# Attention and two dense layers in one program: the order of the first batch is planned anew

## The chip, the cores and the metric

One core of a Trainium2 chip runs the program. The metric is the device time of one execution in microseconds (us); lower is better. The engines are TensorE (PE; its weight loads are shown apart as PEld), VectorE (DVE), ScalarE (ACT), GpSimd (POOL) and the queue of SyncE (SP), which issues nearly all transfers.

## What is computed

The reference takes q, k and v of shape (4, 8, 576, 64), rotates q and k by position, and computes attention for each of 4 batches and 8 heads; its output, as 2304 rows of 512, goes through two dense layers of width 2048 with different gates:

```python
scores = scale * np.matmul(q_rot, k_rot.transpose(0, 1, 3, 2))
attn = np.exp(scores - np.max(scores, axis=-1, keepdims=True))
attn = attn / (np.sum(attn, axis=-1, keepdims=True) + 1e-09)
x = np.matmul(attn, v)              # then (B, S, H * D) as 2304 x 512
h = x @ w_in
x = (h * np.clip(h + 3.0, 0.0, 6.0) / 6.0) @ w_out      # layer 1
h = x @ w_in2
P = a[0] + a[1] * h + a[2] * h ** 2 + a[3] * h ** 3
Q = 1.0 + np.abs(b[0]) * np.abs(h) + np.abs(b[1]) * h ** 2
out = (P / (Q + 1e-06)) @ w_out2                         # layer 2
```

## The kernel before

Heads are handled in pairs, four pairs to a batch. For a pair, `prep_qk` loads q and k, bounds their size, rotates them (L796, L803, L806), splits them into a high and a low 16-bit half (L812) and transposes both by DMA on SP (tiles t0, t1); `prep_v` loads v and splits it (L747). A unit of attention (`unit`) is 128 query rows of both heads of a pair (64 rows of each in the last one). PE makes the scores s (L854), DVE takes the row maximum mx (L860), ACT the exponential e (L867); e is split into p16h (a copy on POOL, ACT or DVE, L537 to L541) and p16l (a subtract on DVE, L879), both are transposed by DMA (L876), and PE multiplies them with v into ob (L896, L899, "pv"). Units 0 and 1 of a pair are part 0 of the batch (256 rows), units 2 to 4 part 1 (320 rows). `x_out` divides by the sum, splits the rows (L923, L932) and transposes them into xt (L935).

Once all four pairs of a part are there, `layer1` runs: for each of 16 slices f of the hidden width 12 matmuls (L966), relu on ACT (L970), the product t on DVE (L972), its high half gh and low half gl (L975); then, for each of four output blocks, four pieces of 12 matmuls (L990) that need the splits of w_out for four slices f each. The weights of layer 1 come as raw float32: 16 slices of w_in and 16 of w_out are loaded (raw, L619 and L622), decoded into an exact scaled form (ACT L634, DVE L636, L637), bounded (L652) and split into two halves (L539 on POOL, L644 on DVE). One scale serves four slices of w_in; all of w_out has one, so no split of w_out can start before its last slice is loaded, decoded and bounded. The splits of w_out carry the name so in the rows. Layer 2 is decoded during the last batches and runs at the end (L1140, L1173).

Nothing of this is issued in the order in which it is written. Every step is an `Op` with a list of engines that may run it, a cost, a priority and its dependences. `Plan.order` plays the program through with these costs: whenever an engine is free it takes the ready step with the lowest priority number; a second choice of engine costs a penalty. The result is the order of instructions on each engine, and each engine then keeps to it. The priority of a step is a time in ticks that `at` sets, plus an offset of its class of tiles from the table `PR` (`o_`, and `z_` for the first batch alone):

```python
o.prio += PR.get("o_" + cls(o.nm[1:]), 0) * 4000
if self.first:
    o.prio += PR.get("z_" + cls(o.nm[1:]), 0) * 4000
```

The other entries of `PR` that matter here: `wi0`, `wi1`, `wo0`, `wo1` set the times at which slices of w_in and w_out are due, `l1o` and `l1p` those of layer 1, `c01` moves part 1 of batch 0, and the `e_` entries list the engines for a class of steps (D, A, G for DVE, ACT, POOL; those that end in 0 hold for the early batches).

Of the kernel before, what the change touches and what calls it, by code (L numbers as in the profile page):

```python
# [37 lines left out]
PR = {'c01': -11.047,  # L38
# [69 lines left out]
 'o_hx': 2.9,
 'o_ident': 123.38,
 'o_k2': 20.73,  # L110
 'o_lgh': 20.57,
 'o_lgl': -106.78,
 'o_lq': -26.42,
 'o_lr': -17.86,
 'o_ls': -32.38,
 'o_lt': 4.62,
# [10 lines left out]
 'o_pth': -0.49,
 'o_ptl': -17.99,
 'o_pw': 29.19,
 'o_pwi': -70.51,  # L130
 'o_qal': -46.2,
 'o_qam': -19.48,
 'o_qb': -31.25,
 'o_qk16': -0.07,
 'o_qpi': -4.09,
 'o_qps': 9.14,
 'o_qpv': -7.12,
 'o_r': -32.53,
# [1131 lines left out]
```

## Time and profile before

| | before |
|---|---|
| time, median of 3 runs | 1168.32 us (1166.86 to 1169.74) |
| profiled execution | 1166.88 us |
| its span, first to last instruction | 1165.1 us |
| mean granted clock of PE | 0.943 |
| busy PE / PEld | 989.7 us (85%) / 787.6 us (68%) |
| busy DVE | 946.6 us (81%) |
| busy ACT | 686.3 us (59%) |
| busy POOL | 227.4 us (20%) |
| DMA queue q1 (SP) | 54.1% of 16 engines' span |

A busy share is an average over stages that differ: where one engine is at 98% another may wait for it, and the roles change with the stage. So the table tells only which engines come into question. The rows further below cut the span at points of the program (the first matmul of layer 1, of its second half, of part 1, of batch 1).

### The profile page before, as it was taken

The page shows a single profiled execution, that of the slowest core. Times are in us where ns is not written, and L with a number is a line of the kernel's source. Part 1 is how long each engine was busy: PE and PEld are TensorE (multiplying, and loading weights), DVE is VectorE, ACT ScalarE, POOL GpSimd, SP SyncE. Part 2 cuts the span into 40 slices and gives each one's busy share as a digit, 9 for nine tenths or more (in the row PEclk, how much of TensorE's full clock was granted, in tenths as well). Part 3 has the DMA queues.
Part 4 walks back from the last instruction along what each step waited for, and adds up shares of the span by engine and source line. Part 5 has one row for each costly group of instructions (what it writes and reads, how often), then busy time and mean ns, then how long its engine had stood idle before and what let it go on. Part 6 is the DMA issues. An engine that isn't in the chain of part 4 may idle for free.

```text
span 1165.1 us, 21501 instructions
## 1 busy us (share of the span) xinstructions
PE 989.7 (85%) x8102; PEld 787.6 (68%) x8102; DVE 946.6 (81%) x1721; ACT 686.3 (59%) x1233; POOL 227.4 (20%) x271
## 2 busy tenths in 40 slices
PE   0222456989998999998999999989999999999997
PEld 0121235876677777777866787768888888888895
DVE  5879789889868789878894747689988889787887
ACT  4545633646446556464654634588776776676676
POOL 0343055433424223243231310000000000000000
PEclk9955566999999999999999999999999999999999
DMA  6888887788689787979889884721210010010010
GB/s 196 222 176 222 199 149 162 154 158 153 121 170 171 154 158 164 180 161 160 173 174 171 164 183 146 260 70 52 81 37 1 25 34 7 1 37 10 1 37 19
DMA packets 299048, 142.97 MB, mean 123 GB/s; under 512 B 246720, under 2 KB 280128, under 8 KB 298944
## 3 DMA queue, kind: packets, MB, share of 16 engines
q1 hardware_dynamic: 293456, 134.69, 54.1%
q10 hardware_dynamic: 5488, 6.92, 2.3%
q8 instruction: 63, 1.03, 0.4%
q14 instruction: 41, 0.34, 0.1%
HBM read 61.33 MB, written 17.83 MB: 68 GB/s over the span
## 4 chain that ended last, share of the span: by engine, by line
PE 53%; DVE 20%; DMA 10%; ACT 6%; issue 5%; SPq 3%; POOL 2%; ACTq 0%; DVEq 0%; POOLq 0%
PE ac L1173 15%; PE h L990 9%; PE hh L1140 9%; PE hx L1140 7%; PE h L966 7%; DMA ptl<-p16l 5%; DVE mx L860 4%; PE s L854 4%; DVE p16l L879 3%; ACT e L867 3%; DMA t<-qk 2%; PE ob L896 2%; DVE w L644 1%; DVE t L972 1%; DVE gl L975 1%
## 5 line engine op out<-in xcount | busy, mean ns | idle before, releaser
L966 PE MATMUL h<-xt,w 128*128 128x256 f16 (+1 forms) x1536 | 202.7, 287 | 8.6 <-DVE t L972 7.5
L990 PE MATMUL h<-gh,w 128*128 128x256 f16 (+1 forms) x960 | 190.6, 287 | 0.0
L1173 PE MATMUL ac<-w,lgh 128*128 128x512 f32 x576 | 179.3, 392 | 3.3 <-ACT lgh L1163 2.5
L966 PEld LDWEIGHTS <-w 128*128 128x128 f16 x1536 | 148.5, 98 | 49.6 <-issue 11.5
L867 ACT ACTIVATE e<-s,mx,qal 128x576 f32<-128x576 f32 (+1 forms) x144 | 116.0, 834 | 104.3 <-DVE p16l L879 49.0
L990 PEld LDWEIGHTS <-w 128*128 128x128 f16 x1440 | 139.3, 99 | 35.2 <-issue 0.3
L854 PE MATMUL s<-t,t 128*128 128x192 f16 (+9 forms) x360 | 88.3, 300 | 65.8 <-DMA t<-qk 28.9
L990 PE MATMUL h<-gl,w 128*128 128x256 f16 (+1 forms) x480 | 137.8, 287 | 0.0
L860 DVE TENSOR_REDUCE mx<-s 128x2 f32<-128x1152 f32 (+1 forms) x80 | 99.4, 1245 | 38.0 <-PE s L854 19.8
L854 PEld LDWEIGHTS <-t 128*128 128x128 f16 (+1 forms) x720 | 61.6, 109 | 100.6 <-issue 43.3
L1173 PEld LDWEIGHTS ac<-w,lgh 128*128 128x128 f32 x576 | 106.9, 188 | 28.1 <-ACT lgh L1163 4.0
L1140 PE MATMUL hh<-x,w 128*128 128x512 f32 (+1 forms) x516 | 117.7, 378 | 2.7 <-DVE lt L1155 2.7
L879 DVE TENSOR_TENSOR p16l<-e,p16h 128x1152 f16<-128x1152 f32 (+1 forms) x80 | 101.2, 1265 | 20.6 <-DMA ptl<-p16l 19.5
L1173 PE MATMUL ac<-w,lgl 128*128 128x512 f32 x288 | 113.0, 392 | 0.0
L1140 PEld LDWEIGHTS hh<-x,w 128*128 128x128 f32 x516 | 92.0, 190 | 23.2 <-DVE lt L1155 3.9
L970 ACT ACTIVATE t<-h,half,d 128x256 f32<-128x256 f32 (+1 forms) x128 | 74.9, 587 | 47.7 <-PE h L966 46.7
L1140 PE MATMUL hx<-x,w 128*128 128x512 f32 (+1 forms) x444 | 98.2, 370 | 0.0
L539 POOL TENSOR_SCALAR gh<-t 128x256 f16<-128x256 f32 (+1 forms) x95 | 66.2, 698 | 148.6 <-DVE t L972 143.7
L862 POOL TENSOR_SCALAR mx<-mx,qal 128x2 f32<-128x2 f32 (+1 forms) x75 | 53.4, 712 | 203.3 <-DVE mx L860 140.2
L1140 PEld LDWEIGHTS hx<-x,w 128*128 128x128 f32 x444 | 77.5, 188 | 16.0
L854 PE MATMUL s<-k,t 128*128 128x192 f16 (+9 forms) x360 | 85.2, 299 | 0.0
L896 PE MATMUL ob<-v,pth 128*128 128x65 f16 (+1 forms) x800 | 77.1, 200 | 7.2 <-DMA pth<-p16h 3.3
(132 smaller groups left out, 1938.4 us busy)
## 6 DMA issues: line engine op xcount, KB each, us to landing
raw<-in_moe_w_in_dram SPq DMA_DIRECT2D x32, 512.0 KB, 4.7
raw<-in_moe_w_out_dram SPq DMA_DIRECT2D x32, 512.0 KB, 4.3
w2d<-f SPq DMA_DIRECT2D x32, 256.0 KB, 4.3
w2s<-w2d SPq DMA_DIRECT2D x32, 256.0 KB, 2.8
out_dram<-ob SPq DMA_DIRECT2D x36, 128.0 KB, 2.4
vnat<-in_v_dram SPq DMA_DIRECT2D x16, 256.0 KB, 3.4
nat<-in_q_dram SPq DMA_DIRECT2D x32, 128.0 KB, 2.4
nat<-in_k_dram SPq DMA_DIRECT2D x32, 128.0 KB, 2.5
```

The lines of the kernel that those rows point to most:

```text
L539: pool.tensor_scalar(out, in_, scale, 0.0, ALU.mult, ALU.add)
L854: pe.matmul(sbank()[r0:r0 + m, x:y], lhsT=qq[:, q0:q0 + m], rhs=kk[:, kx:kx + y - x], start=(j == 0), stop=(j == 1))
L860: op("D", c_dve(n), lambda e: vec.reduce_max(mx()[:, 0, 0:g], sv().rearrange("p (g n) -> p g n", g=g), axis=AX.X), r=[s], w=[(mx, 0)])
L862: op(EN("e_mx"), {"D": 170, "G": 270}, lambda e: EL[e].tensor_scalar(mx()[:, 1, 0:g], mx()[:, 0, 0:g], al()[:, 1:2], float(LSH * np.log(2. ...
L867: op("A", c_act(n // g, 2, False), lambda e, h=h: act.activation(et()[:, h * (n // g):(h + 1) * (n // g)], sv()[:, h * (n // g):(h + 1) * ...
L879: op(EN("lo"), c_sub(n), lambda e: EL[e].tensor_tensor(lo()[:, 0:n], et()[:, 0:n], ph()[:, 0:n], ALU.subtract), r=es + [ph], w=[lo])
L896: pe.matmul(ob()[0:m, o:o + D + 1], lhsT=w, rhs=vv[:, 0], start=(z == 0 and j == 0), stop=(z == 1 and j == 4))
L966: pe.matmul(hp()[:, 0:N], lhsT=w[:, z, kk], rhs=xt()[:, kk, 0:N], start=(n == 0), stop=(n == 11))
L970: op("A", c_act(N, 2, False), lambda e, t=t, hp=hp, f=f: act.activation(t()[:, 0:N], hp()[:, 0:N], AF.Relu, bias=half(), scale=d()[:, f:f ...
L990: pe.matmul(yp()[:, 0:N], lhsT=w[:, s_, m * 128:(m + 1) * 128], rhs=gt()[:, f, 0:N], start=(f == 0 and z == 0), stop=(f == KF - 1 and z == 2))
L1140: pe.matmul(hp()[:, 0:n], lhsT=w[:, kk], rhs=xt()[:, kk, 0:n], start=(i == 0), stop=(i == 11))
L1173: pe.matmul(accs[j][i]()[0:m], lhsT=gt()[:, x:x + m], rhs=wt(), start=(f == 0 and z == 0), stop=(f == KF - 1 and z == 2))
```

## The change

The table `PR` has new values nearly throughout, two new entries, and the preparation of the first batch reads them. Pairs 1 to 3 of batch 0 were due 4 ticks apart and before pair 0's time; now all four pairs start at one time of their own, one `step0` apart. v of pair 0 (`s0`) is due early, not late. Part 1 of batch 0 is moved ahead by 1 tick instead of 11 (`c01`). The offsets `z_` of the first batch are new and nearer to zero. Some engine lists change: the maxima's scaling (`e_mx`) runs on POOL alone outside the early batches, v's copy (`e_v`, `e_v0`) has POOL or DVE as its first choice instead of ACT, layer 1's output (`e_y`) stays on ACT.

```diff
-PR = {'c01': -11.047,
+PR = {'c01': -1.023,
...
- 'e_hi': 'GAD',
+ 'e_hi': 'ADG',
  'e_hi0': 'ADG',
- 'e_mx': 'DG',
+ 'e_mx': 'G',
...
- 'e_v': 'AD',
- 'e_v0': 'AG',
+ 'e_v': 'DG',
+ 'e_v0': 'GAD',
...
- 'e_y': 'AD',
+ 'e_y': 'A',
...
+ 'lead0': 7.701,
...
- 's0': 11.806,
+ 's0': -13.557,
...
+ 'step0': 0.971,
...
         if b_ == 0:
-            at(0)
+            at(-PR["lead0"])
             prep_qk(0)
             at(PR["s0"])
             prep_v(0)
             for p in range(1, HP):
-                at(4 * p - PR["lead"])
+                at(PR["step0"] * p - PR["lead0"])
                 prep_qk(p)
                 prep_v(p)
```

What the planner makes of it is seen in the order of instructions. The new kernel's table is two lines longer, so a line of it has a number that is 2 higher: L974 there is L972 here.

The first place is DVE's list just ahead of the first product t of layer 1. Before:

```order
L922 RECIPROCAL r<-r 128x6
L919 TENSOR_TENSOR xf<-vqs,vpv 128x1
L923 TENSOR_TENSOR xu<-xu,r 128x6x64
L609 RECIPROCAL qps<-qpv 128x2
L747 SCALAR_TENSOR_TENSOR v_90<-vnat_85,vqs,v_90 128x10x64
L932 TENSOR_TENSOR xl<-xu,xh 128x384
L972 SCALAR_TENSOR_TENSOR t<-t,h 128x256
```

The same place now:

```order
L639 SCALAR_TENSOR_TENSOR w_9_1306<-raw,w_9_1306 128x512
L638 TENSOR_SCALAR w_10_1330<-w_10_1330 128x512
L639 SCALAR_TENSOR_TENSOR w_10_1330<-raw,w_10_1330 128x512
L974 SCALAR_TENSOR_TENSOR t<-t,h 128x256 x2
L977 TENSOR_TENSOR gl<-t,gh 128x256
L862 TENSOR_REDUCE mx<-s 128x2
L974 SCALAR_TENSOR_TENSOR t<-t,h 128x256
L638 TENSOR_SCALAR w_11_1387<-w_11_1387 128x512
L881 TENSOR_TENSOR p16l<-e,p16h 128x1152
```

Before, the first t stood behind x_out of part 1 of the first pair (r, xu, xl) and behind all 16 splits of w_out, the last of which is in the next fence. Now t comes while the slices of w_out are still being decoded (w_10 here), and no split of w_out stands ahead of it.

The second place is DVE's list at the last split of w_out (w_14). Before:

```order
L644 SCALAR_TENSOR_TENSOR w_11_1451<-w_12_961,so,w_11_1451 128x512
L541 COPY xu<-ob 128x130
L860 TENSOR_REDUCE mx<-s 128x1
L644 SCALAR_TENSOR_TENSOR w_12_1461<-w_13_986,so,w_12_1461 128x512
L932 TENSOR_TENSOR xl<-xu,xh 128x256
L796 SCALAR_TENSOR_TENSOR ropea<-nat,tab 128x18x32
L860 TENSOR_REDUCE mx<-s 128x2
L644 SCALAR_TENSOR_TENSOR w_13_1479<-w_14_996,so,w_13_1479 128x512
L605 TENSOR_SCALAR qpi<-ob 128x2
L879 TENSOR_TENSOR p16l<-e,p16h 128x1152
L644 SCALAR_TENSOR_TENSOR w_14_1524<-f_1007,so,w_14_1524 128x512
```

Now:

```order
L646 SCALAR_TENSOR_TENSOR w_11_2295<-w_12_1462,so,w_11_2295 128x512
L881 TENSOR_TENSOR p16l<-e,p16h 128x1152
L646 SCALAR_TENSOR_TENSOR w_12_2335<-w_13_1557,so,w_12_2335 128x512
L798 SCALAR_TENSOR_TENSOR ropea<-nat,tab 128x18x32
L862 TENSOR_REDUCE mx<-s 128x2
L646 SCALAR_TENSOR_TENSOR w_13_2357<-w_14_1585,so,w_13_2357 128x512
L805 TENSOR_TENSOR nat<-nat,tab 128x1152
L646 SCALAR_TENSOR_TENSOR w_14_2379<-f_1647,so,w_14_2379 128x512
L881 TENSOR_TENSOR p16l<-e,p16h 128x640
```

Before, the last splits stood ahead of the first t, among attention and the loads' scaling. Now they stand behind all 16 products t of part 0, between part 1's attention and the rotation of the next batch's q and k (ropea, nat).

The third place is SP's list, where loads of w_out (raw) end. Before:

```order
L935 DMA_TRANSPOSE xt_906<-xh 128x2x128
L935 DMA_TRANSPOSE xt_922<-xl 128x2x128
L622 DMA raw<-in_moe_w_out_dram 128x1024 x2
L876 DMA_TRANSPOSE ptl<-p16l 128x9x128
L622 DMA raw<-in_moe_w_out_dram 128x1024
L876 DMA_TRANSPOSE pth<-p16h 128x9x128 x2
```

Now, around the transposes xt of the fourth pair:

```order
L937 DMA_TRANSPOSE xt_766<-xh 128x2x128
L878 DMA_TRANSPOSE ptl<-p16l 128x9x128
L624 DMA raw<-in_moe_w_out_dram 128x1024
L937 DMA_TRANSPOSE xt_783<-xl 128x2x128
L624 DMA raw<-in_moe_w_out_dram 128x1024 x2
L878 DMA_TRANSPOSE pth<-p16h 128x9x128
L878 DMA_TRANSPOSE ptl<-p16l 128x5x128
```

The first of these fences shows the second pair's transposes (xt_906 and xt_922, high and low half) and the last three loads of w_out, which stood ahead of the third pair's. Now the fourth pair's transposes (xt_766, xt_783) come while w_out is still loaded; six of its loads stand behind them, between transposes of p16h and p16l.

## Rows read from the trace of the kernel before

**Rows 1.** The page's slices: PE's busy tenths and its granted clock, in 40 equal parts.

```profile
PE   0222456989998999998999999989999999999997
...
PEclk9955566999999999999999999999999999999999
```

**Rows 2.** Windows by stage: length, busy us (count) of each engine, PE clock, DMA share, GB/s.

```profile
0.00:189.50 189.50, 57.78 (x499) 41.97 (x499) 149.39 (x289) 91.61 (x185) 62.51 (x67) 0.68 0.79 192
189.50:225.70 36.20, 34.08 (x398) 28.20 (x397) 33.98 (x69) 21.41 (x43) 17.34 (x24) 0.96 0.83 153
225.70:265.00 39.30, 34.53 (x406) 28.80 (x403) 34.23 (x55) 19.79 (x35) 14.27 (x13) 1.00 0.84 154
265.00:338.00 73.00, 68.82 (x747) 50.94 (x746) 60.42 (x109) 37.69 (x67) 26.98 (x30) 1.00 0.80 148
338.00:690.00 352.00, 330.57 (x3779) 263.85 (x3777) 276.39 (x520) 193.62 (x324) 103.95 (x136) 1.00 0.86 168
690.00:1165.10 475.10, 463.87 (x2288) 373.86 (x2286) 392.21 (x683) 322.23 (x581) 2.40 (x3) 0.99 0.19 52
```

**Rows 3.** Timeline of PE: start, us, instruction; the firsts of L966, L990, part 1, batch 1.

```profile
189.54 4.34 PE L966 MATMUL h<-xt,w 128*128 128x256 f16 x24
...
225.71 0.27 PE L990 MATMUL h<-gh,w_s 128*128 128x256 f16 x1
...
264.94 0.30 PE L966 MATMUL h<-xt,w 128*128 128x320 f16 x1
...
337.88 1.47 PE L966 MATMUL h<-xt,w 128*128 128x256 f16 x12
```

**Rows 4.** Windows, 30 to 190 us.

```profile
30.00:190.00 160.00, 56.90 (x498) 41.10 (x499) 133.53 (x241) 78.69 (x156) 62.58 (x64) 0.62 0.81 191
```

**Rows 5.** Groups, first 189.5 us: busy us, mean ns | idle before, releaser.

```profile
L637 DVE SCALAR_TENSOR_TENSOR w<-raw,w 128x512 int32<-128x512 int32 x31 | 22.1, 732 | 0.2
...
L644 DVE SCALAR_TENSOR_TENSOR w<-w,so,w 128x512 f16<-128x512 f32 x14 | 12.6, 900 | 3.8 <-POOL w L539 3.8
...
L636 DVE TENSOR_SCALAR w<-w 128x512 int32<-128x512 int32 x31 | 12.4, 417 | 9.8 <-ACT w L634 9.8
```

**Rows 6.** Groups, whole run: maxima, subtracts, t and gl on DVE.

```profile
L879 DVE TENSOR_TENSOR p16l<-e,p16h 128x1152 f16<-128x1152 f32 x64 | 87.9, 1374 | 16.0 <-DMA ptl<-p16l 14.9 <-POOL p16h L539 1.0
...
L860 DVE TENSOR_REDUCE mx<-s 128x2 f32<-128x1152 f32 x64 | 86.3, 1352 | 26.0 <-ACT e L867 14.3 <-PE s L854 8.9 <-ACT t L970 2.4
...
L975 DVE TENSOR_TENSOR gl<-t,gh 128x256 f16<-128x256 f32 x64 | 30.4, 487 | 1.9 <-POOL gh L539 1.9
...
L972 DVE SCALAR_TENSOR_TENSOR t<-t,h 128x256 f32<-128x256 f32 x64 | 26.1, 412 | 5.8 <-ACT t L970 5.6
```

**Rows 7.** Timeline of DVE: a split, the instruction behind it, and the last split.

```profile
175.51 1.62 DVE L644 SCALAR_TENSOR_TENSOR w<-w,so,w 128x512 f16<-128x512 f32 x1 [0.59 <-POOL w L539]
177.05 1.34 DVE L806 TENSOR_TENSOR nat<-nat,ropea 128x1152 f32<-128x1152 f32 x1
...
189.61 0.75 DVE L644 SCALAR_TENSOR_TENSOR w<-f,so,w 128x512 f16<-128x512 f32 x1 [0.59 <-POOL w L539]
```

**Rows 8.** Timeline of PE: a score unit, a unit of pv and 48 matmuls of L966 begin.

```profile
201.49 0.40 PE L854 MATMUL s<-t,t 128*64 128x512 f16 x1
...
202.63 0.20 PE L896 MATMUL ob<-v,pth 128*128 128x65 f16 x1
...
203.58 5.77 PE L966 MATMUL h<-xt,w 128*128 128x256 f16 x48
```

**Rows 9.** Groups, whole run: the copies p16h on POOL.

```profile
L539 POOL TENSOR_SCALAR p16h<-e 128x1152 f16<-128x1152 f32 x32 | 41.7, 1304 | 22.4 <-ACT e L867 16.5 <-POOL gh L539 2.1 <-issue 1.9
```

**Rows 10.** Timelines of POOL and DVE: a copy, a subtract beside it, a subtract alone.

```profile
139.83 1.15 POOL L539 TENSOR_SCALAR p16h<-e 128x1152 f16<-128x1152 f32 x1 [1.53 <-ACT junk L652]
...
139.88 2.31 DVE L879 TENSOR_TENSOR p16l<-e,p16h 128x1152 f16<-128x1152 f32 x1
...
146.07 1.35 DVE L879 TENSOR_TENSOR p16l<-e,p16h 128x1152 f16<-128x1152 f32 x1
```

More of the change, by code (lines that the diff above doesn't have):

```diff
@@ L106 @@
- 'o_hh': 3.47,
+ 'o_half': 66.6,
+ 'o_hh': 3.05,
  'o_hr': 11.75,
[L108 to L116, printed above, removed]
+ 'o_hx': 2.17,
+ 'o_ident': 138.79,
+ 'o_k2': 20.81,
+ 'o_lgh': 53.65,
+ 'o_lgl': -159.43,
+ 'o_lq': -53.65,
+ 'o_lr': -2.25,
+ 'o_ls': -34.29,
+ 'o_lt': 4.25,
  'o_mx': 12.06,
- 'o_na': 32.3,
- 'o_nat': 5.5,
+ 'o_na': -45.2,
+ 'o_nat': 6.15,
  'o_ob': -0.02,
- 'o_ones': 67.22,
+ 'o_ones': 72.16,
@@ L122 @@
  'o_p1': -5.5,
  'o_p16': 0.25,
- 'o_p16h': 71.26,
- 'o_p16l': 0.03,
+ 'o_p16h': 32.49,
+ 'o_p16l': 0.33,
  'o_pt': 6.74,
[L127 to L138, printed above, removed]
+ 'o_pth': -4.52,
+ 'o_ptl': -9.92,
+ 'o_pw': 35.47,
+ 'o_pwi': -44.5,
+ 'o_qal': -73.87,
+ 'o_qam': -26.95,
+ 'o_qb': -48.22,
+ 'o_qk16': 4.58,
+ 'o_qpi': -3.4,
@@ L180 @@
+ 'o_vps': -35.07,
+ 'o_vpv': -77.42,
+ 'o_vqi': 6.84,
+ 'o_vqs': -58.99,
+ 'o_vqv': -17.48,
+ 'o_vv': -17.75,
+ 'o_w0_': 40.8,
+ 'o_w1_': 9.73,
+ 'o_w2_': 9.9,
+ 'o_w2d': 62.1,
+ 'o_w2s': -18.87,
+ 'o_wam': -39.02,
+ 'o_wao': 5.69,
+ 'o_woi': -107.17,
+ 'o_wos': 20.49,
+ 'o_wov': 44.65,
+ 'o_wpi': -154.61,
+ 'o_wps': -23.23,
+ 'o_x20': 116.02,
+ 'o_x21': -0.5,
+ 'o_xf': 11.26,
+ 'o_xh': -33.15,
+ 'o_xl': 14.95,
  'o_xn': -19.23,
- 'o_xt': -5.19,
- 'o_xu': -1.53,
+ 'o_xt': -11.36,
+ 'o_xu': -8.64,
@@ L188 @@
  'p16l': 1,
- 'pen': 7.889,
+ 'pen': 7.418,
  'pm': 0,
  'pt': 2,
- 'pv': 5.327,
- 'q_k2': 'AQ',
+ 'pv': 6.419,
+ 'q_k2': 'QA',
  'q_nat': 'Q',
@@ new lines @@
+ 'z_f32': 8.07,
+ 'z_g2h': 0.0,
+ 'z_gh': -14.04,
+ 'z_gl': -0.51,
+ 'z_h': 0.0,
+ 'z_h2': 0.0,
+ 'z_half': -10.82,
+ 'z_hh': -8.5,
+ 'z_hr': 0.0,
+ 'z_hx': 3.93,
+ 'z_ident': -8.76,
+ 'z_k2': 26.21,
+ 'z_lgh': -1.25,
+ 'z_lgl': 17.55,
+ 'z_lq': 6.06,
+ 'z_lr': -1.93,
+ 'z_ls': -16.45,
+ 'z_lt': -3.17,
+ 'z_mx': -0.03,
+ 'z_na': -20.82,
+ 'z_nat': -0.01,
+ 'z_ob': 0.06,
+ 'z_ones': -25.61,
+ 'z_p1': 0.0,
+ 'z_p16': 0.0,
+ 'z_p16h': -11.01,
+ 'z_p16l': 0.0,
+ 'z_pt': 0.0,
+ 'z_pth': 0.89,
+ 'z_ptl': -8.13,
@@ new lines @@
+ 'z_pw': 2.56,
+ 'z_pwi': -3.9,
+ 'z_qal': 0.48,
+ 'z_qam': 3.82,
+ 'z_qb': -8.89,
+ 'z_qk16': -5.39,
+ 'z_qpi': 6.81,
+ 'z_qps': -13.66,
+ 'z_qpv': -1.31,
+ 'z_r': 5.16,
+ 'z_r0': 0.0,
+ 'z_raw': 3.72,
+ 'z_ropea': 0.0,
+ 'z_s': 0.0,
+ 'z_so': 2.72,
+ 'z_t': -13.02,
+ 'z_t0': 2.23,
+ 'z_t1': -0.22,
+ 'z_tab': 1.34,
+ 'z_u': 0.0,
+ 'z_v9': -0.53,
+ 'z_vam': 22.59,
+ 'z_vm4': -1.37,
+ 'z_vnat': 0.0,
+ 'z_vnat0': -0.34,
+ 'z_vnat1': 11.21,
+ 'z_vpi': 3.94,
+ 'z_vps': 2.18,
+ 'z_vpv': -0.76,
+ 'z_vqi': 0.09,
@@ L321, in cls @@
+ 'z_vqs': -3.6,
+ 'z_vqv': -0.13,
+ 'z_vv': 0.0,
+ 'z_w0_': -1.91,
+ 'z_w1_': -1.69,
+ 'z_w2_': -11.93,
+ 'z_w2d': -53.68,
+ 'z_w2s': 0.31,
+ 'z_wam': 0.46,
+ 'z_wao': -23.4,
+ 'z_woi': -19.0,
+ 'z_wos': -20.61,
+ 'z_wov': -28.27,
+ 'z_wpi': 19.44,
+ 'z_wps': 3.61,
+ 'z_x20': -25.98,
+ 'z_x21': -5.61,
+ 'z_xf': 0.57,
+ 'z_xh': -0.37,
+ 'z_xl': -1.14,
+ 'z_xn': 0.0,
+ 'z_xt': -3.31,
+ 'z_xu': 0.87,
+ 'z_y0': 0.0,
+ 'z_y1': 0.65,
+ 'z_y1d': 19.64}
 def cls(nm):
```

208 lines of the change are left out of this document (51 added, 157 removed).

## The prediction

> **What bounds the kernel now.** I read the page's slices first. The TensorE (PE) line climbs from 0 to 9 over the first seven slices [rows 1] (29 us each), and the granted clock stands at 0.5 to 0.6 of full speed in four of them; from the eighth slice on PE is at 8 or 9 to the end. So the time lost lies in the first 200 us. The table by stages [rows 2] says how much: in the first 189.5 us, up to the first matmul of layer 1 (L966) [rows 3], PE is busy 57.8 us, VectorE (DVE) 149.4, ScalarE (ACT) 91.6, GpSimd (POOL) 62.5. From 30 to 190 us DVE is busy 133.5 of 160 us, a share of 0.83 [rows 4]. No other compute engine is near that, so DVE's list paces the start, with waits on transfers and on POOL in between. The next two stages, layer 1's first half for part 0 of batch 0 (to 225.7 us) and its second half (to 265.0), have DVE at 34.0 of 36.2 and 34.2 of 39.3: still DVE, with PE close behind. From 265 to 338 us (part 1 of batch 0, up to batch 1's first L966) it turns: PE 68.8 of 73.0 (0.94), DVE 60.4 (0.83). From 338 us on PE has 0.94 and then 0.98 [rows 2], and nothing but PE's own work is left. A gain must therefore come before about 265 us, and what is won there is kept, as far as DVE lets PE keep it.
>
> **The change, step by step.** It is a new order; the tiles, the arithmetic and the number of matmuls are the same. So I ask at three places how much work stands ahead on the pacing engine, and price it by rows of before.
>
> *First place: the first L966.* Counted over the whole order of DVE, the new list has 50 instructions fewer ahead of the first product t (L972, which reads the first L966). All 16 splits of w_out move behind it: 16 x 0.90 = 14.4 us [rows 5]. So do 5 decodes, 5 x (0.42 + 0.73) = 5.8 [rows 5], one row maximum and one low-half subtract, 1.35 + 1.37 = 2.7 [rows 6], and 22 other instructions, x_out steps of part 1 and small scale steps, of which I price the large ones like the rows nearest in width (three of about 0.9, four of about 0.45) and the rest at 0.15: some 7 us. The sum is 30 us of records. A record overlaps the next by some 0.08 us (175.51 + 1.62 against a start at 177.05 [rows 7]), so 26 us of DVE's time go. Divided by its share of 0.83 that is 31 us: the first L966 comes at 158 us instead of 189.5. The bounds: 189.5 if the transposes on SP hold it, 158 if DVE alone decides. SP's list speaks for 158: ahead of the fourth pair's transposes it now has 10 loads of w_out instead of 16, and three transposes of p16h and p16l fewer.
>
> *Second place: the last split of w_out.* Layer 1's second half (L990) needs it for its last four f. In before it ended at 190.4 us [rows 7], long ahead of its first use at 225.7 [rows 3]. Now it stands behind all 16 products t and 16 low halves gl of the part, 16 x (0.41 + 0.49) = 14.4 us, 7 row maxima and 7 subtracts, of which two each are narrower and priced by their width (five of 1.35 and two of 0.75, 8.3 us; five of 1.37 and two of 0.76, 8.4 us) [rows 6], and 12 us of x_out, loads' scaling and small steps: 43 us more of records, 76 instructions, 37 us after overlap. DVE's work up to there is then 150 + 37 = 187 us. It has done 149.4 - 26 = 123 at 158 us, so 64 us are left; at a share of 0.90, between the 0.94 and 0.87 of the two stages [rows 2], these take 71 us: the last split ends at 229 us, not 190. PE by then stands further on than it did at 229 us in before, since the order interleaves two output blocks and starts them on the first splits. Behind the last split PE has 10 pieces of 12 matmuls, 3 score units and 4 units of pv before part 1's first L966. A piece takes 1.44 us (48 in 5.77), a score unit 1.14 (201.49 to 202.63), pv 0.95 (202.63 to 203.58) [rows 8]: 14.4 + 3.4 + 3.8 = 21.6 us, at PE's 0.88 of that stage 25 us. So part 1 starts at 254 us instead of 264.9 [rows 3], 11 us early. DVE's list gives 9: ahead of the 17th t it has 9.7 us of records less, 7.7 net, over 0.87. Lead: 10 us.
>
> *Third place: batch 1's first t.* There DVE's list is only 4.7 us shorter (3.9 net; six copies xu and a p16h that other engines take, a decode and a qk split that come later). If DVE paced this stage at its 0.83, the lead would shrink to 3.9 / 0.83 = 5 us. If PE paces it, the 10 us stay: DVE would have 60.4 + 7.7 - 3.9 = 64.2 us in 73, a share of 0.88, which it exceeded in the stage from 189.5 on. I take 8 us, nearer to PE's end, as PE is the one at 0.94.
>
> *Later batches and layer 2.* The engine choices move 11 copies p16h and 10 copies v from ACT to POOL, which costs POOL some 27 us, the 1.30 of a p16h each [rows 9]; POOL has 104 of 352 us there [rows 2], so ACT and PE wait for none of it as long as POOL is idle when they come. I cost them at nothing; if that cover goes, the second rival below has the price. PE's order in layer 2 differs in a few places and ends with the same rows; at 0.98 I give it nothing, either way.
>
> **Sum.** The profiled execution took 1166.88 us (span 1165.1 and 1.8 around it). 1166.9 - 8 = 1158.9. The median of the three runs shown is 1168.32, 1.4 above it, so I predict **1160.3 us**; this case spans a lead of 5 to 10 us with some 2 us for the rest, 1156 to 1165.
>
> The Trainium skill, "SBUF — State Buffer", section "Who interferes with whom", has a rule that speaks against this change: a DVE instruction with two SBUF inputs and a GpSimd instruction that reads SBUF take turns on one shared port pair, whole instructions at a time. The trace agrees: a subtract p16l that began 0.05 us after a POOL copy of 1.15 us took 2.31 us, another took 1.35 [rows 10]. By this rule every moved copy can stretch a DVE instruction, and the sum would be that of the second rival.
>
> **The rivals.**
> 1. *PE runs free from the first L966 (more gain).* PE has 34.1 + 34.5 + 68.8 = 137 us of work from there to batch 1 [rows 2]. Were DVE able to keep 0.94 (its share from 189.5 to 225.7) over the 151 us that it then has (278 - 4 up to 338 us, less 123), batch 1 would start at 158 + 161 = 319 us, 19 us early: 1149. For it: DVE held 0.94 once. Against it: that was 36 us only. Chance 0.15.
> 2. *The lead is eaten (no change).* Up to batch 1's start about ten more copies stand on POOL. Each that meets a two-input DVE instruction costs DVE up to 2.31 - 1.35 = 0.96 us [rows 10], 10 x 0.96 = 9.6 us on the engine that paces, against a lead of 8: 1168.3 + 1.6 = 1170; at half the meetings 1165. For it: DVE is the pacing engine just there. Against it: the mean p16l is 1.37 [rows 6], so most miss each other. Chance 0.18.
> 3. *The splits of w_out come too late (slower).* The first split needs the scale of the whole matrix, so the last load, and 6 of the 16 loads now stand behind the fourth pair's transposes on SP, between transposes that wait for p16h and p16l. In the sum the last split ends at 229 us; each us later moves part 1, and from 239 us on the change loses. If the loads and with them the splits come 20 us later, the last at 249 us, the lead of 10 becomes a loss of 10; 2 us more because PE idles in front of L990 and comes back at the lower clock, where 12 matmuls take 2.17 us (24 in 4.34 [rows 3]) instead of 1.44, for three pieces: 1168.3 + 12 = 1180. For it: loads and transposes share SP's queue in order. Against it: before's last split was 35 us early. Chance 0.20.
>
> The clock stands at its lower level (1.2 GHz) in slices with PE at 2 to 5 tenths and at the upper (2.4 GHz) in those with 8 or 9 [rows 1]. The Trainium skill, "TensorE: Matmul & The Clock Gate", section "HAM oscillation — how this bites in real kernels", says that waits between short bursts of matmuls bring the slower clock back each time; that would make the third rival's price a repeated one.
>
> **How the numbers follow.** My forecast has 0.47, the rivals 0.15, 0.18 and 0.20. A measurement of this kernel can tell about 0.3% (3.5 us) from no change, so "same" is 1164.8 to 1171.8. The forecast and the first rival give faster, 0.61 with a small part of the forecast's upper end taken off; same gets the second rival and that part, 0.19; slower the third, 0.20. The range from 1147 to 1173 holds the forecast, the second rival, most of the first and the mild end of the third.
>
> **What would show it.** Right: the first L966 near 158 us (up to 170 would do), the last split of w_out at 225 to 235, part 1's first L966 near 255, batch 1's near 330, and equal stages behind it. Wrong: the first L966 early but batch 1's first one at 338 or later (the lead was eaten: look for p16l well over 1.4 us), L990 waiting for splits past 240 us at half clock, or a difference that arises after 338 us.

## The result, and the profile after

The changed kernel takes 1156.29 us (median of 4 runs, 1154.58 to 1157.46), the kernel before on the same chip 1168.69 (4 runs, 1166.86 to 1169.74): a ratio of 0.9886 with an interval from 0.9864 to 0.9908. It is faster by 12.4 us; the forecast said 8. The profiled execution after took 1157.46 us, its span 1155.4, which is 9.7 us less than before's span; the mean granted clock is 0.959 (before 0.943).

The page's slices of the changed kernel, PE's busy tenths and granted clock in 40 equal parts (28.9 us each):

```profile
PE   1243577788998898999989999989999999999997
...
PEclk9976598899999999999999999999999999999999
```

Against [rows 1] PE stands at 4, 3, 5, 7 and 7 in the third to seventh slice, where it had 2, 2, 4, 5 and 6, and is a little emptier in the eighth, tenth, fourteenth and sixteenth (7, 8, 8 and 8, where 9 stood). The windows by stage, cut at the same points of the program as [rows 2], say where the time went (length, busy us and count of each engine, PE's clock, DMA share, GB/s):

```profile
0.00:145.40 145.40, 50.88 (x428) 36.90 (x429) 116.28 (x242) 73.51 (x150) 45.53 (x48) 0.78 0.85 204
145.40:196.20 50.80, 37.10 (x437) 30.77 (x437) 48.27 (x89) 32.10 (x69) 29.21 (x33) 0.94 0.90 179
196.20:244.50 48.30, 40.39 (x455) 32.82 (x455) 40.58 (x61) 20.11 (x36) 26.49 (x23) 0.87 0.74 155
244.50:321.70 77.20, 69.00 (x724) 50.41 (x721) 66.57 (x120) 40.11 (x76) 32.29 (x35) 1.00 0.73 147
321.70:688.70 367.00, 339.83 (x3862) 272.43 (x3860) 285.08 (x524) 184.03 (x320) 107.70 (x148) 0.99 0.85 166
688.70:1155.40 466.70, 455.60 (x2209) 365.68 (x2206) 388.97 (x675) 321.53 (x581) 2.40 (x3) 0.99 0.19 53
```

The points themselves, PE's first L968 (L966 before), first L992 (L990), part 1's and batch 1's first L968, as in [rows 3] (timeline of PE: start, us, instruction):

```profile
145.38 1.86 PE L968 MATMUL h<-xt,w 128*128 128x256 f16 x9
...
196.21 0.37 PE L992 MATMUL h<-gh,w_s 128*128 128x256 f16 x1 [1.94 <-DVE t L974]
...
244.50 1.79 PE L968 MATMUL h<-xt,w 128*128 128x320 f16 x12
...
321.71 1.47 PE L968 MATMUL h<-xt,w 128*128 128x256 f16 x12
```

| point | before | after | lead | lead in the forecast |
|---|---|---|---|---|
| first L966/L968 of batch 0 | 189.5 | 145.4 | 44.1 | 31 |
| first L990/L992 | 225.7 | 196.2 | 29.5 | not given |
| part 1's first L966/L968 | 264.9 | 244.5 | 20.4 | 10 |
| batch 1's first | 337.9 | 321.7 | 16.2 | 8 |
| batch 2's first | 488.8 | 481.3 | 7.5 | 8 |
| batch 3's first | 636.7 | 624.8 | 11.9 | 8 |
| last matmul of layer 1 | 756.6 | 746.4 | 10.2 | 8 |
| span | 1165.1 | 1155.4 | 9.7 | 8 |

A lead of 44 us appears at the first L968, 24 of it are paid back by the time part 1 starts, since w_out's splits now lie in that stretch, and of the remaining 20 half is gone by the end of layer 1. DVE's timeline has the last split of w_out, and the windows around its end (223.2 us) the load of both engines (columns as above; PE, PEld, DVE, ACT, POOL):

```profile
222.40 0.75 DVE L646 SCALAR_TENSOR_TENSOR w<-f,so,w 128x512 f16<-128x512 f32 x1 [0.87 <-POOL w L541]
```

```profile
0.00:223.20 223.20, 107.64 (x1082) 83.14 (x1083) 186.40 (x367) 116.19 (x236) 91.34 (x95) 0.82 0.84 192
145.40:223.20 77.80, 56.76 (x656) 46.24 (x656) 70.11 (x126) 42.68 (x86) 45.81 (x47) 0.89 0.82 171
223.20:244.50 21.30, 20.73 (x241) 17.35 (x239) 18.74 (x24) 9.53 (x18) 9.88 (x8) 0.95 0.84 156
```

### The profile page after: what moved, and what is told of

It reads as the page before. It is cut to its first block, busy times and chain, and to the rows that moved or that the text cites. A ratio compares the mean times of both kernels' runs of the same rounds, so it can differ in the third digit from the quotient of the medians.

```text
span 1155.4 us, 21512 instructions
## 1 busy us (share of the span) xinstructions
PE 992.8 (86%) x8102; PEld 789.0 (68%) x8102; DVE 945.8 (82%) x1707; ACT 671.4 (58%) x1230; POOL 243.6 (21%) x288
## 5 line engine op out<-in xcount | busy, mean ns | idle before, releaser
L968 PE MATMUL h<-xt,w 128*128 128x256 f16 (+1 forms) x1536 | 204.7, 289 | 12.7 <-DVE t L974 12.6
L992 PE MATMUL h<-gh,w 128*128 128x256 f16 (+1 forms) x960 | 191.6, 288 | 1.0 <-DVE w L646 1.0
L968 PEld LDWEIGHTS <-w 128*128 128x128 f16 x1536 | 149.9, 99 | 53.8 <-issue 14.7
L992 PEld LDWEIGHTS <-w 128*128 128x128 f16 x1440 | 139.6, 99 | 37.3 <-DVE w L646 1.3
L992 PE MATMUL h<-gl,w 128*128 128x256 f16 (+1 forms) x480 | 138.2, 288 | 0.0
L856 PE MATMUL s<-t,t 128*128 128x192 f16 (+9 forms) x360 | 88.8, 302 | 50.8 <-ACT e L869 28.9
L881 DVE TENSOR_TENSOR p16l<-e,p16h 128x1152 f16<-128x1152 f32 (+1 forms) x80 | 102.2, 1277 | 12.3 <-DMA ptl<-p16l 12.1
L972 ACT ACTIVATE t<-h,half,d 128x256 f32<-128x256 f32 (+1 forms) x128 | 74.8, 586 | 52.7 <-PE h L968 49.6
L864 POOL TENSOR_SCALAR mx<-mx,qal 128x2 f32<-128x2 f32 (+1 forms) x80 | 57.7, 721 | 172.0 <-DVE mx L862 132.6
L898 PE MATMUL ob<-v,pth 128*128 128x65 f16 (+1 forms) x800 | 77.3, 200 | 11.8 <-DMA pth<-p16h 10.5
L541 POOL TENSOR_SCALAR gh<-t 128x256 f16<-128x256 f32 (+1 forms) x90 | 56.9, 636 | 130.9 <-DVE t L974 124.1
```

What stands on the lines that cost most here:

```text
L541: pool.tensor_scalar(out, in_, scale, 0.0, ALU.mult, ALU.add)
L856: pe.matmul(sbank()[r0:r0 + m, x:y], lhsT=qq[:, q0:q0 + m], rhs=kk[:, kx:kx + y - x], start=(j == 0), stop=(j == 1))
L864: op(EN("e_mx"), {"D": 170, "G": 270}, lambda e: EL[e].tensor_scalar(mx()[:, 1, 0:g], mx()[:, 0, 0:g], al()[:, 1:2], float(LSH * np.log(2. ...
L881: op(EN("lo"), c_sub(n), lambda e: EL[e].tensor_tensor(lo()[:, 0:n], et()[:, 0:n], ph()[:, 0:n], ALU.subtract), r=es + [ph], w=[lo])
L898: pe.matmul(ob()[0:m, o:o + D + 1], lhsT=w, rhs=vv[:, 0], start=(z == 0 and j == 0), stop=(z == 1 and j == 4))
L968: pe.matmul(hp()[:, 0:N], lhsT=w[:, z, kk], rhs=xt()[:, kk, 0:N], start=(n == 0), stop=(n == 11))
```

## The experiments

Three questions were open. Is the gain the shorter list of DVE ahead of the first L966, as the forecast had it, so that the amount of work counts? Is it the place of w_out's splits? Or is it all the new order of batch 0 together? And does anything behind batch 1's start matter? All kernels but the two originals share one edit, which makes the order a table of its own instead of the planner's answer:

```diff
-    res = pl.order()
+    res = [(pl.ops[i], chr(e)) for i, e in struct.iter_unpack("<HB", zlib.decompress(base64.b85decode(ORDER)))]
```

`ORDER` lists every step and its engine. It is made by sorting the steps by a key, as far as their dependences allow; the keys are the planned starts of the two kernels ("old" and "new"), changed as each diff says.

**Halves of the two plans, put together.** The first pair takes batch 0's steps from one plan and the rest from the other; to close the gap between them, the old plan's starts are taken 20.5 us earlier.

```diff
-key = new[step]
+key = new[step] if step.first else old[step] - 20.5     # e1; e2 with old and new exchanged
```

> The first batch (its loads, weights of layer 1, attention, layer 1: 893 of 4344 steps) in the changed kernel's order, all other steps in the old kernel's order and on its engines. Theory A, the gain is made in the first batch and about 6 us of it are lost later by the new order of the later steps: batch 1's first L966 near 322 us as in the changed kernel, and a time of 1150 to 1154 us. Theory B, the gain comes from the order and engines of the later batches: 1164 to 1169 us. If the later steps do not matter at all: 1156 us.

> The other half: the first batch in the old kernel's order, all other steps in the changed kernel's order and on its engines. Theory A: batch 1's first L966 near 338 us as in the old kernel, and a time of 1169 to 1175 us. Theory B: 1155 to 1160 us. If the later steps do not matter at all: 1168 us.

Measured: 1171.3 us for new batch 0 with old rest, a ratio of 1.002 (0.9998 to 1.0042), and 1198.67 for old with new, 1.0248 (1.0205 to 1.0291). (The kernel before took between 1168.57 and 1171.43 us on the chips of these experiments; a ratio is always to the kernel before on the same chip, and ratios, not times, are compared across experiments.) Both times miss every range that was expected. In the first, L966 begins at 154.9 us but part 1 only at 269.9; in the second at 196.3 and 288.1. Neither is evidence on a part of the change: batch 0's steps share every queue with the preparation of batch 1, and the shift by 20.5 us set that preparation among them at places that neither plan has, which is the likely reason but was not traced. What they show is that in such an order a start of 155 us is worth nothing by itself. The next experiments therefore keep a plan whole and move few steps, or cut it at one point.

**Cut at batch 1's first L966.** One plan is taken word for word up to that step (1272 of 4344 steps for the new one), the other plan's order behind it.

```diff
-key = (0, new_position[step])
+key = (0, new_position[step]) if new_position[step] < cut else (1, old_position[step])     # e7; e8 exchanged
```

> A cleaner cut than the first two runs: the changed kernel's order, word for word, up to batch 1's first L966 (1272 of 4344 steps), and behind it all remaining steps in the old kernel's order and on its engines (the two kernels' sets of steps ahead of that point differ by 20). Theory A, the whole gain is made ahead of that point and some 6 us of it are lost by the new later order: batch 1's first L966 at 320 to 324 us, time 1149 to 1153 us. If the later order is neutral: 1155 to 1158. Theory B, the later order makes the gain: 1164 or more.

> The other half of the clean cut: the old kernel's order up to batch 1's first L966, then the changed kernel's order and engines. Theory A: first L966 of batch 1 at 336 to 342 us, time 1171 to 1176 us. If the later order is neutral: 1167 to 1170. Theory B: 1156 to 1160.

Measured: new up to batch 1, then old: 1155.19 us, 0.9873 (0.9858 to 0.9889), the whole gain. Old up to batch 1, then new: 1173.63, 1.0041 (1.0026 to 1.0056), a loss. So the gain is made ahead of batch 1's start, and the new order behind it adds nothing: the first time lies in the range of a later order that is neutral (1155 to 1158 us), the second in that of one that costs some (1171 to 1176). The windows from batch 1's first L966 to layer 1's last matmul, first the kernel before:

```profile
337.90:756.60 418.70, 397.26 (x4267) 313.72 (x4265) 320.24 (x610) 222.93 (x373) 106.36 (x139) 1.00 0.82 172
```

The changed kernel:

```profile
321.70:746.40 424.70, 397.53 (x4269) 314.47 (x4267) 324.98 (x606) 212.74 (x368) 110.11 (x151) 0.99 0.82 172
```

New start with old rest:

```profile
323.30:747.40 424.10, 400.13 (x4267) 315.11 (x4267) 322.37 (x613) 222.38 (x372) 105.39 (x139) 0.99 0.82 173
```

Old start with new rest:

```profile
339.40:762.80 423.40, 396.50 (x4266) 313.82 (x4265) 320.63 (x602) 212.62 (x367) 111.14 (x151) 1.00 0.81 170
```

The stretch takes 418.7 us only where both are old. The new start alone makes it 424.1, the new rest alone 423.4, both together 424.7, with 396.5 to 400.1 us of PE's work in all four. So going back to the old order behind batch 1 would not bring back the 6 us of lead that are lost there; they are lost behind the new start with either order. PE's waits from batch 1's first L966 to batch 2's grow from 10.5 to 15.2 us, those for DVE from 5.5 to 10.8 of them (us in total, times, longest; the main rows). Before:

```profile
PE s L854 <- ACT e L867: 2.2, 3, 1.4
...
PE h L966 <- DVE t L972: 1.8, 3, 1.0
PE s L854 <- DVE mx L860: 1.2, 2, 0.7
...
```

After:

```profile
PE h L968 <- DVE t L974: 4.7, 4, 2.2
PE s L856 <- ACT e L869: 3.6, 3, 1.3
PE s L856 <- DVE mx L862: 2.9, 2, 2.5
...
```

DVE has done 278.0 us of work at batch 1's start before [rows 2] and 271.7 after: PE arrives 16.2 us earlier, DVE's work by less, and PE then waits for t and mx. That this is the reason for the 6 us was not isolated, and it can't be for the old start with the new rest: there PE arrives no earlier (339.4 us, DVE at 278.0 again), and the stretch is as long.

**The moved copies on their old engines.** The changed kernel's order, with the 126 steps behind batch 0 that changed engine put back.

```diff
-engine = new_engine[step]
+engine = old_engine[step] if not step.first else new_engine[step]
```

> The changed kernel's order; outside the first batch the 126 steps that the change gave to another engine run on the old kernel's engine at the same place (copies p16h and v back from GpSimd to ScalarE among them). If those moved copies cost the 6 us of lead that are lost between batch 1's start and the end of layer 1: 1149 to 1153 us. If they cost nothing: 1155 to 1158. If the order only fits its own engines: 1159 or more.

Measured: 1158.09 us, 0.9907 (0.9887 to 0.9926), against 0.9886 for the change: the same within the intervals. The copies of p16h and v that went from ACT to POOL behind batch 0 cost nothing and bring nothing that these runs can tell, and are not where the lead goes: batch 1 begins at 322.1 us here and layer 1 ends at 747.6, 425.5 us as against 424.7.

**w_out's splits put back ahead of the first L966.** The changed kernel with all loads, decodes, copies and splits of w_out set earlier in the plan, the last split at 165 us of it, and the 16 first L968 set behind the splits in the sorting.

```diff
-key = new[step]
+key = a0 + (new[step] - a0) * (165 - a0) / (a1 - a0) if step in w_out else new[step]     # a0, a1: first and last of w_out
```

> The changed kernel's order with one part undone: all loads, decodes and splits of w_out stand ahead of the first L966 again, all else in the changed kernel's order. Theory A, VectorE paces up to part 1 and its work there is the same in either order: the first L966 comes 25 to 35 us later (170 to 180 us), part 1's first within 5 us of the changed kernel's 244.5, and the time within 4 us of its 1156 (1154 to 1160). Theory C, it is the early start of layer 1 that brings the gain (TensorE has matmuls in its empty stretch and keeps the upper clock): part 1's first L966 at 255 or later and a time of 1164 to 1168 us.

Measured: 1185.31 us, 1.0139 (1.0098 to 1.018). L966 begins at 196.0 us, L990 at 224.1, part 1 at 271.6, 27.1 later than in the change, and layer 1 ends 25.9 us later. Its windows from 145 us on:

```profile
145.00:196.00 51.00, 19.71 (x209) 14.74 (x208) 39.03 (x60) 16.47 (x32) 23.24 (x25) 0.57 0.59 124
196.00:224.00 28.00, 27.19 (x279) 23.02 (x277) 19.72 (x43) 14.35 (x30) 11.35 (x19) 0.95 0.36 74
224.00:271.60 47.60, 39.25 (x459) 32.20 (x457) 34.70 (x52) 20.07 (x36) 15.60 (x14) 0.89 0.91 169
```

First DVE works 39 of 51 us and PE 20, at a granted clock of 0.57; then PE works 27.2 of 28 and DVE 19.7. In the change the stretch from 145.4 to 196.2 has both at once, DVE 48.3 and PE 37.1 of 50.8. DVE's work up to part 1 is 206.7 us here and 205.1 in the change, so the 27 us are not work: DVE's phase and PE's stand one behind the other instead of side by side. (The transfers run unevenly too: the DMA share is 0.59 and 0.36 in the first two stretches and 0.91 in the third.) The theory that only DVE's amount of work counts falls here; the other one had the direction, and a loss that was too small (1164 to 1168 us expected). The edit moves loads and decodes as well as splits, so it does not tell them apart; the next ones do.

**Only the last decodes put back.** The splits stay; the last 4 decodes and bounds of w_out, and all 16 loads, come ahead of the first L968, which is set behind them in the sorting.

```diff
-key = new[step]
+key = a0 + (new[step] - a0) * (148 - a0) / (a1 - a0) if step in w_out_decodes else new[step]
```

> The changed kernel with the last 4 decodes and bounds of w_out, and so all 16 of its loads, ahead of the first L966, which waits for them in the plan; the 16 splits stay at the changed kernel's places. A middle step between it and the kernel in which the splits stand ahead too (time 1185.3, first L966 at 196 us). If each us of start that is lost is kept to the end: the first L966 at 155 to 170 us and the time later by as much, 1166 to 1180 us. If only the overlap of the splits counts, and PE waits for them in layer 1's second half anyway (it idles 13.7 us between 145 and 196 us): first L966 at 150 to 170 us, but L990 at 196 to 200 us, part 1 at 243 to 249 us, time 1155 to 1160 us.

Measured: 1175.53 us, 1.003 (1.0006 to 1.0054). (The trace is of a run of 1170.72 us, one of the fastest of 12.) L968 begins at 169.5 us, 24 later than in the change; the last split ends at 238.2 (+15.0), part 1 begins at 259.0 (+14.5), layer 1 ends at 760.5 (+14.1). So a part of the late start is made up (L992 has idle time in front of it), and from the last split on the loss is kept to the end. So the loads and decodes alone, ahead of the first L968, cost 14.5 of the 27.1 us at part 1's start, and more than the whole gain at the end.

**The splits later.** The changed kernel, copies and splits of w_out 20 us later in the plan.

```diff
-key = new[step]
+key = new[step] + 20 if step in w_out_splits else new[step]
```

> The changed kernel with the 16 copies and 16 splits of w_out set 20 us later in the plan: 25 to 29 rows later in DVE's list, the last one just ahead of the 17th t. Third rival of the prediction (each us by which the last split comes later moves part 1 by one): the last split ends at 233 to 243 us instead of 223, part 1's first L966 comes at 254 to 264 us instead of 244.5, and the time is 1164 to 1175 us. The other theory (PE has attention of part 1 and of batch 1 to do meanwhile, and the total work of both engines up to batch 1 sets its start): part 1 later by under 5 us, batch 1 at 320 to 326 us, time 1154 to 1160 us.

Measured: 1177.35 us, 1.0052 (1.0034 to 1.007). It is the third rival in kind, but the last split and part 1 lie beyond its ranges (31 us and 21.8 us later instead of 10 to 20), and each us of the last split moved part 1 by 0.7, not by one. The timeline of DVE has the first and the last split, the windows the stretch from 190.3 us, about the last L968 of part 0, to part 1, PE's waits what it mostly stood for:

```profile
199.87 0.74 DVE L736 SCALAR_TENSOR_TENSOR w_s<-w,so,w_s 128x512 f16<-128x512 f32 x1
...
253.61 0.74 DVE L736 SCALAR_TENSOR_TENSOR w<-f,so,w 128x512 f16<-128x512 f32 x1
```

```profile
190.30:266.30 76.00, 46.23 (x478) 36.36 (x477) 54.28 (x75) 22.34 (x39) 39.06 (x32) 0.80 0.60 119
```

```profile
PE s L946 <- ACT e L959: 8.5, 3, 6.0
PE s L946 <- DVE mx L952: 6.4, 2, 4.3
PE ob L750 <- ACT junk L744: 5.1, 1, 5.1
PE h L1082 <- DVE w L736: 3.2, 2, 2.0
...
```

The last split ends 31 us later (254.4), part 1 begins 21.8 later (266.3), layer 1 ends 21.7 later (768.1). PE waits for the splits themselves for 3.2 us only. For most of the rest it stands in front of scores whose e, mx and bounds are late. Only w_out's copies and splits were moved, so those waits follow from them through the engines' fixed lists; an engine's idle time carries the name of the last link, not of the cause.

**The splits earlier.** The 16 splits at half their spacing, the last 16 rows earlier in DVE's list.

```diff
-key = new[step]
+key = t0 + (new[step] - t0) / 2 if step in w_out_splits else new[step]     # t0: the first of them
```

> The changed kernel with the 16 copies and splits of w_out at half their spacing in the plan: the first stays, the last is 16 rows earlier in DVE's list (row 328 instead of 344), between the products t of part 0. If the last split still sets part 1's start (as it did when it came 31 us later and moved part 1 by 22): last split at 210 to 216 us instead of 223, part 1's first L966 at 234 to 240 us instead of 244.5, time 1147 to 1153 us. If the changed kernel's place already leaves it idle slack and a split put between two t only delays t by its own length: layer 1's first half ends 2 to 6 us later than 190.2 us, part 1 at 242 to 250 us, time 1155 to 1161 us.

Measured: 1166.66 us beside 1170.72 for the kernel before, 0.9955 (0.9936 to 0.9973). The last split ends at 211.5 us, 11.7 earlier, but layer 1's first half ends at 197.4 (change: 191.4; the 190.2 of the expectation is 1.2 us too early), L992 begins at 204.7 (196.2), part 1 at 250.1 (+5.6), and layer 1 ends 10.8 us later. The window, and the largest row of PE's waits in it:

```profile
145.00:196.00 51.00, 40.30 (x418) 31.95 (x417) 46.58 (x85) 29.84 (x64) 27.45 (x34) 0.83 0.80 172
```

```profile
PE h L1058 <- DVE t L1064: 5.7, 5, 2.2
```

In the change PE has 443 matmul records in the same 51 us at a clock of 0.94, here 418 at 0.83. Up to 180 us, where the orders are the same, both have 300; the 25 are lost behind it, among the splits. PE's waits for t are 2.9 us in the change, so a split between two t may delay the next matmuls; but all of PE's waits in the window are 10.7 us here and 11.8 there, and how much of the loss is the lower clock was not separated. The first expectation fell (an earlier last split did not bring part 1 forward); the second had the first half's delay (6.0 us) and part 1 (250.1) at or just past its upper ends, and a time below the measured one (0.9955 is 1163.4 us on the first chip). So of the three places that were tried for the splits the change has the best: they lose when they come earlier and when they come later.

**w_out late, all else old.** The converse of the third experiment: the kernel before, w_out's steps where the new plan has them between the steps of layer 1.

```diff
-key = old[step]
+key = interpolate(new[step], new_milestones, old_milestones) if step in w_out else old[step]
```

> The kernel before with one thing moved: the loads, decodes, copies and splits of w_out stand where the changed kernel has them, relative to the steps of layer 1 (12 of 16 loads and 27 of 31 decodes on DVE ahead of the first t, all 16 splits behind it; the first t is row 255 of DVE's list instead of 289). Everything else, x_out of part 1 ahead of the first t too, stays. Theory C (the gain is the overlap of w_out's splits with layer 1's first half, whatever the rest of the order): the first L966 of batch 0 comes ahead of 170 us, part 1's ahead of 252 us, batch 1's ahead of 328 us, and the time is 1155 to 1160 us. Theory D (the splits are only half of it; the nearly equal due times of the four pairs are needed too, since pair 3's attention still ends late): the first L966 at 175 to 190 us, part 1 at 256 us or later, time 1162 to 1169 us.

Measured: 1188.29 us, 1.0137 (1.0116 to 1.0159). L966 begins at 182.8 us, part 1 at 287.1, batch 1 at 359.0. Both theories were too hopeful. DVE's groups from 145 to 183 us (busy us, mean ns | idle before, releaser) name what it lacks:

```profile
L969 DVE TENSOR_TENSOR p16l<-e,p16h 128x1152 f16<-128x1152 f32 (+1 forms) x5 | 6.2, 1247 | 5.3 <-DMA ptl<-p16l 5.3
...
L902 DVE SCALAR_TENSOR_TENSOR qk<-nat,qps,qk 128x576 f16<-128x576 f32 x2 | 2.5, 1250 | 4.5 <-POOL qk L629 4.5
```

It stands for 12.4 of 38 us (25.60 busy; 33.01 before and 36.50 in the change), with no split and no t in its list to fill them: PE still has attention ahead of its first L966 (up to 182.8 us, 11.9 of these 38 us waiting for ptl), and the splits are no longer there for DVE to do meanwhile. Then they come late as well (the last ends at 264.8 us). With the third experiment this makes a square:

| | w_out's steps early (old) | late (new) |
|---|---|---|
| the other steps old | 1 | 1.0137 |
| the other steps new | 1.0139 | 0.9886 |

Either part of the change alone loses 1.4%, both together gain 1.1%. (The two mixed orders are not plans that a planner made; others with the same parts could lose less. "The other steps" are all the rest of the order, the near-equal due times of the pairs among them; no run moves those alone.)

**POOL's copies of w_in and w_out on ACT.** Two kernels take the high-half copies away from POOL, at the same places of the order: the kernel before with the 16 of w_in on ACT, and the changed one with the 16 of w_out.

```diff
-engine = old_engine[step]
+engine = ACT if step in w_in_copies and old_engine[step] == POOL else old_engine[step]     # e5: w_out_copies, new
```

> The old kernel's order with the 16 high-half copies of w_in on ScalarE instead of GpSimd, each at the same place of the order. Theory D, these copies on GpSimd stretched VectorE's low-half subtracts beside them from 0.74 to 1.04 us, and that this is gone explains 5 us of VectorE's time in the changed kernel: the 16 subtracts of w_in fall to a mean of 0.74 to 0.80 us, the first L966 comes 5 us earlier, and the time is 1163 to 1166 us. The rival, the stretch lies beside other waits and costs nothing: 1167 to 1170 us though the subtracts are shorter; or they stay at 1.04 us because something else stretched them.

> The changed kernel with the 16 high-half copies of w_out on ScalarE instead of GpSimd, each at the same place. GpSimd takes 26 of 48 us in the stage of layer 1's second half, ScalarE 20. If GpSimd's copies pace the splits: the last split ends 5 us or more before 223 us, part 1 starts 3 to 6 us earlier, and the time is 1150 to 1153 us. If VectorE's own list paces them, as I hold after the run with w_in's copies on ScalarE changed nothing: 1154 to 1158 us, with the last split within 3 us of 223.

Measured: 1168.11 us, 0.9984 (0.9959 to 1.0009), no difference from before; and 1156.64, 0.9891 (0.9878 to 0.9905), none from the change (its last split begins at 223.56 us instead of 222.40). The first is the more telling. The group of w_in's subtracts up to 132 us (min/median/max ns, first and last start), before:

```profile
L644 DVE SCALAR_TENSOR_TENSOR w<-w,wps,w x16: 739/1172/1226, 34.2 to 89.4; 128x512 f16<-128x512 f32 x16
```

With the copies on ACT:

```profile
L734 DVE SCALAR_TENSOR_TENSOR w<-w,wps,w x16: 730/745/752, 33.9 to 88.7; 128x512 f16<-128x512 f32 x16
```

```profile
30.00:190.00 160.00, 58.55 (x497) 42.12 (x498) 128.09 (x241) 88.00 (x172) 47.30 (x48) 0.63 0.82 191
```

DVE is busy 128.1 us there instead of 133.5 [rows 4], and the first L966 comes at 189.8 us as before (189.5). The 5 us came back as waiting, and the larger part of it as waiting for the moved copies themselves, a row that the kernel before does not have (DVE's waits from 30 to 189.8 us):

```profile
DVE w L734 <- ACT w L627: 3.2, 7, 1.1
```

ACT has 9.3 us more to do in the stretch (88.0 instead of 78.7). So DVE's busy time beside POOL's copies was partly waiting, and shortening it bought nothing; but as ACT got the work, the run does not prove that DVE's list is not what paces the start.

**All kernels side by side.** Windows from 0 to part 1's first L966, by when each kernel has done the same matmuls of batch 0 part 0 and all splits:

| kernel | part 1 starts | DVE busy | DVE idle | layer 1 ends |
|---|---|---|---|---|
| changed | 244.5 | 205.1 | 39.4 | 746.4 |
| splits earlier | 250.1 | 206.0 | 44.1 | 757.2 |
| last decodes early | 259.0 | 206.9 | 52.1 | 760.5 |
| before | 264.9 | 217.5 | 47.4 | 756.6 |
| splits later | 266.3 | 211.2 | 55.1 | 768.1 |
| w_out early, rest new | 271.6 | 206.7 | 65.0 | 772.3 |
| w_out late, rest old | 287.1 | 214.5 | 72.6 | 778.0 |

Within the new order the work differs by 6 us at most and the start by 27: what an edit of the order changes is idle time. Against before, 12.4 of the 20.4 us are busy time of DVE that is gone ahead of part 1 (4.4 of it the shorter subtracts of w_in, see below), and 8.0 idle time.

## Why the prediction was right, point by point

The direction and the stage were right. That the end came out near is in part luck: the forecast's own span was 1156 to 1165 us and 1156.29 lies at its lower edge, the lead at batch 1's start was twice the forecast, and a loss behind it that the forecast had at nothing took most of the excess back. Of its own signs, the first L966, the last split, part 1 and batch 1 all came earlier than named, and a difference did arise after 338 us.

1. *What bounds the kernel.* That the gain is made ahead of batch 1's start is shown: all of it stays with the old order behind that point (0.9873); the lead of 20.4 us at 244.5 us puts it ahead of part 1. That DVE's list paces the start, because no other compute engine has its share, is not shown. The prediction passes over the transfers, and no run separates them from DVE. Their share of the DMA engines is 0.81 where DVE has 0.83 [rows 4], and 0.87 beside 0.87 in the change (the window from 30 to 145 us below). Up to the first L966 they moved 36.4 MB before (189.5 us at 192 GB/s) and 29.7 MB in the change (145.4 us at 204). At before's rate 29.7 MB take 154 us, an estimate that is nearly as good as the 150 us from DVE's list in point 2. With the last decodes put back they moved 34.2 MB by 169.5 us (202 GB/s). PE's waits for transfers from 30 us to the first L966 fell from 43.9 to 12.3 us. The two largest before (us in total, times, longest):

```profile
PE s L854 <- DMA t<-qk: 28.9, 4, 10.3
...
PE ob L896 <- DMA ptl<-p16l: 11.7, 5, 5.4
```

   After:

```profile
PE ob L898 <- DMA pth<-p16h: 10.5, 1, 10.5
...
PE ob L898 <- DMA ptl<-p16l: 1.8, 2, 1.3
```

   A transfer can be late because SP's queue is full or because its input is late, so this does not decide between the two; it stays open what paces the first 145 us. Two readings of the slices were wrong: the granted clock is at 5 or 6 tenths in five of them, not four, and in the second PE has 2 tenths at a clock of 9 [rows 1].
2. *First place, 158 us forecast, 145.4 measured.* The term "26 us of DVE's time go" was too small: 149.4 - 116.3 = 33.1 went. Some 4.4 of the missing 7 are w_in's 16 subtracts (15.7 us busy before, 11.3 now), which the forecast left at their length; they take 738 ns on average now and 1041 before, most likely since POOL's copies of w_in begin at 28.1 us and the subtracts only at 60.4, and no longer go each beside the other:

```profile
L646 DVE SCALAR_TENSOR_TENSOR w<-w,wps,w x16: 733/737/745, 60.4 to 108.6; 128x512 f16<-128x512 f32 x16
```

   With 33.1 / 0.83 the forecast's rule gives 150 us; the rest is a higher share, 0.87 from 30 to 145 us:

```profile
30.00:145.00 115.00, 47.57 (x413) 34.09 (x414) 99.89 (x182) 57.77 (x117) 41.67 (x41) 0.73 0.87 198
```

   The rule itself, DVE's list divided by its old share, is weak: for the kernel with w_in's copies on ACT it gives 5.4 / 0.83 = 6.5 us, and that got none, with the waits for ACT named above.
3. *Second place, last split at 229 us forecast, 223.2 measured; part 1 at 254, measured 244.5.* DVE has done 186.4 us of work at the end of the last split (forecast 187), but that agreement is luck: 116.3 us of it ahead of the first L968 (forecast 123) and 70.1 behind (forecast 64), two errors that cancel. The share is 70.11 / 77.80 = 0.90 from the first L968 (forecast 0.90), and behind the split PE has 20.73 us of work (forecast 21.6). PE does it in 21.3 us, at 0.97, where 0.88 was taken. So the 9.5 us are a start that came 12.6 earlier, 6.8 of which the added work took back (6.1 / 0.90), and 4 us of PE's share.
4. *Third place and behind.* A lead of 8 to 10 kept to the end was forecast. The lead was 16.2 at batch 1's start and 10.2 at the end of layer 1. "Equal stages behind it" is wrong: batch 1 to the end of layer 1 takes 424.7 us instead of 418.7, with PE waiting more for DVE in batch 1; why is open (see the cut at batch 1). The end agrees with the forecast since twice the lead arose and two fifths of it were lost.
5. *The moved copies at nothing*: shown for those behind batch 0, within the intervals, by the kernel with the old engines (0.9907).
6. *The rivals.* PE running free (batch 1 at 319 us) was nearly reached at that point, 321.7, but its gain was not kept. The eaten lead fell, at least as the meeting of POOL's and DVE's instructions: p16l and its 640-wide form take 1259 ns on average up to 245 us, against 1295 up to 265 us before. Late splits did not happen, but their price is real: 31 us later moved the end of layer 1 by 21.7. On a line between the change (0.9886 at 223.2 us) and that kernel (1.0052 at 254.4) the gain is gone at a last split of 245 us, an estimate; the prediction had 239. Whether the clock repeats its price there, no run isolates: the granted clock was 0.80 from 190.3 to 266.3 us in that kernel, and 0.87 from 196.2 to 244.5 in the change.

What the prediction did not see is the coupling. It treated w_out's steps as work that moves from one place to another; the square above shows that moving them alone costs 1.4% (16 us), and that the rest of the new order without it costs as much.

## What to carry to other kernels

Where an engine's list is in order, price a move by what fills the engine while it waits: a block of weight preparation went well beside the phase that another engine bounds, but only where the earlier phase was ready in time, so here both had to move together. A busy share of 0.83 is no proof that an engine paces, the less so where the transfers have the same share; take work away from it in one run without giving it to an engine that it then waits for, and if the end stands still, look for the chain that it waits for. Follow a lead to the end of the program before pricing it: here 44 us became 20, 16 and 10.

## What was not expected of the hardware

A DVE subtract with two SBUF inputs (128x512) took 1172 ns at the median while POOL copied slices of the same size beside them, and 745 ns with those copies on ACT, at the same places in the order; POOL's copies beside them had a median of 1115 ns, and 692 ns in the changed kernel, where the subtracts come later. The Trainium skill, "SBUF — State Buffer", section "Who interferes with whom", says that such a DVE instruction and a GpSimd instruction that reads SBUF lock a shared port pair against each other; this pair of runs agrees, at 1.57 times the length. Moving the copies to ACT did not move the end at all (0.9984), with part of the time gone into waits for ACT.
